# A new step order, a split load of q and a last product in two column halves, in an attention and token-mixing kernel on one core

## The chip, the cores and the metric

The kernel runs on one core of a Trainium2 chip. The metric is the device time of one execution in microseconds (us), lower is better. Times of a kernel are given as the median over several runs, and a separate profiled execution has its own time and a span, which is the part of it that the trace covers. Five engines work in parallel, each through its own queue in program order: PE (TensorE, matrix products, results in PSUM), DVE (VectorE), ACT (ScalarE), POOL (GpSimd) and SP (SyncE, here only for issuing DMAs).

## The reference

Eight batches, eight heads, 576 tokens, head size 64, 32 packing queries. Two attentions one after the other, then a token-mixing layer on the heads laid side by side (x is 576 x 512 in each batch):

```python
p_packed = sm_attn(p, k, v)                # softmax(p k^T / 8) v : 32 x 64 per head
out = sm_attn(q, p_packed, p_packed)       # softmax(q p_packed^T / 8) p_packed
x = out.transpose(0, 2, 1, 3).reshape(B, S, H * D)
W_tok = scale * np.einsum('bsd,btd->bst', x @ w_q, x @ w_k)
mixed = np.einsum('bst,btd->bsd', W_tok, x)
return np.maximum(mixed, 0.0) @ w_out      # 8 x 576 x 512, float32
```

## The kernel before

Inputs are float32 in device memory; POOL's DMAs convert them to bf16 while loading. There is no scheduler: a string named ORDER (line 12) lists all steps, and the program issues them in that order, so each engine's queue is the list cut down to that engine's steps. A step is written as NAME.batch.part@engine=PSUM banks, where V is DVE, A is ACT, P is POOL, S is SP. Semaphores for the data follow from what is read and written; an engine whose next step isn't ready stands still, whatever comes after.

The steps of one batch, in order of data, with the lines of their code:

- LD (157 to 184): LD.k, LD.v (two DMAs), LD.q are the batch's loads; LD.g and LD.h are the two halves of k of batch 0; LD.O is w_out, LD.W the two small weights, LD.P p. All but some of P and W go through POOL's queue. Four buffers each for k, q and v (NL).
- KT (256, DVE): k transposed in 32x32 blocks. S1 (264, PE): p k^T. X1 (288, ACT): exp. TE (296, DVE): transposes that exp, from batch 3 on. PV (301, PE): times v, with a column of ones for the sums. RC, PP (313, 317, DVE): reciprocal, scaling, block mask. PT (322, DVE): transposes the result.
- QK, QKE, QD (327 to 341): p_packed times [w_k, w_q] on PE, its eviction, a copy on POOL.
- QV (347, DVE, three parts): q transposed; parts 0 and 1 each read one half of the q tile, part 2 both. S2 (360, PE): scores of q. X2 (373, ACT): exp. RS, RR (388, 394, DVE), AM (399, DVE or POOL): row sums, reciprocals, product. A number behind the batch picks token tiles (TCH): 3 is the first four tiles of 128, 2 the fifth, 4 all, 0 and 1 two each.
- AT (407, PE) and AE (414): the softmax weights transposed. WKQ (426, PE), WE (449): x w_k and x w_q in one go. GM, GE, Y, YE (454 to 479): a 512-row mixing matrix, reduced to 64 x 128 pieces through p_packed. MX and MR (481, 487, PE): mixed, four token tiles and the remainder. RL, RLF, RLR (508 to 515): relu to SBUF.
- OT (520, PE): relu times w_out, four 128x512 products for each of the token tiles 0 to 3; OT.b.4, for odd b, is the remainder of two batches. OE (538) evicts two tiles at once, OEF (541) one. ST (547) stores two tiles in 512 KB or a remainder in 256 KB; STF (565) one tile in 256 KB.
- HOLD (559): a 128-byte DMA on SP that reads a loaded tile. SP can issue nothing behind it until that load has landed; all stores stand behind it in SP's queue. WARM (588): products on a constant, which keep PE busy while it has no data; 74 of them.

PSUM has eight banks of 512 float32 columns; a step that writes a bank waits until the last reader of it is done.

The loads stand in POOL's queue as g h q0 v0 k1 v1 q1 k2 v2 q2 k3 O v3 q3 k4 q4 v4 k5 q5 v5 k6 v6 q6 k7 q7 v7, with POOL's other steps between. Stores go through SP's queue in the order of the list, but for two STF of the last batch on ACT's queue. PE's list from S1.3 to S1.4, and its end:

```
S1.3 MX.1.0 MR.1 MX.1.1 OT.0.0 OT.1.4 OT.0.1 PV.3 AT.2.3 OT.0.2 AT.2.2 OT.0.3 WKQ.2 S2.3 GM.2 OT.1.2 S1.4
...
MX.7.1 MR.7 MX.7.0 OT.6.3 OT.7.4 OT.7.1 OT.7.3 OT.7.0 OT.7.2
```

Of the kernel before, what the change touches and what calls it, by code (L numbers as in the profile page):

```python
# [7 lines left out]
NL, NB, NO, NE = 4, 3, 6, 2  # L8
# [16 lines left out]
PT.2@V RLR.0@V QV.2.1@V RL.0.1@A WARM.2=1 WKQ.1.0=4,5 WKQ.1.2 WKQ.1.1 S2.2.2=2,3 S2.2.3=6,7 WE.1.2@A
GM.1=4 QK.2=5 KT.3.2@V GE.1@V X2.2.3@A X2.2.2@A Y.1=4 QKE.2@V YE.1@A RS.2.4@V S1.3=6,7,0,1 X1.3.0@A
MX.1.0=4,5 MR.1=2,3 RLR.1@A X1.3.1@A TE.3.0@V RR.2.4@V LD.q4 QD.2@P LD.v4 AM.2.2@P LD.k5 LD.q5
MX.1.1=6,7 OT.0.0=2,3 OT.1.4=0 OT.0.1 RL.1.0@A OE.0.0@A TE.3.1@V AM.2.3@V PV.3.0=4,5 PV.3.1 RL.1.1@V
AT.2.3=1 AE.2.3@A OT.0.2=2,3 AT.2.2=6 AE.2.2@A OEF.1.4@V RC.3.1@V RC.3.0@V OT.0.3 OE.0.1@A PP.3.0@V
QV.3.2@V PP.3.1@V QV.3.1@V PT.3@V QV.3.0@V WKQ.2.0=4,5 KT.4.2@V WKQ.2.2 WKQ.2.1 WE.2.2@A S2.3.3=0,1  # L30
S2.3.2=2,3 X2.3.3@A X2.3.2@A GM.2=6 OT.1.2=4,5 S1.4=0,1,2,3 RS.3.4@V GE.2@A Y.2=6 OT.1.3 X1.4.0@A
X1.4.1@A YE.2@A RR.3.4@V QV.4.0@V TE.4.0@V AM.3.2@P QV.4.2@V TE.4.1@V OT.1.0=0,1 MX.2.1=2,3 QK.3=6
QKE.3@V QV.4.1@V OE.1.1@A MR.2=4,5 RLR.2@A RL.2.1@A OT.1.1 PV.4.0=4,5 PV.4.1 AT.3.2=2 MX.2.0=6,7
OE.1.0@A LD.v5 AM.3.3@P LD.k6 QD.3@P LD.v6 RC.4.0@V RC.4.1@V AT.3.3=3 PP.4.0@V PP.4.1@V PT.4@V
AE.3.3@V AE.3.2@A S2.4.2=4,5 RL.2.0@A X2.4.2@A S2.4.3=0,1 QK.4=6 X2.4.3@A KT.5.2@V QKE.4@A RS.4.4@V
RR.4.4@V WKQ.3.0=4,5 WKQ.3.1 WKQ.3.2 OT.2.0=2,3 S1.5=0,1,6,7 WE.3.2@A X1.5.1@A X1.5.0@A OT.2.2=4,5
OT.2.3 GM.3=0 OT.2.1 LD.q6 AM.4.3@P LD.k7 QD.4@P LD.q7 AT.4.3=1 QV.5.1@V TE.5.0@V TE.5.1@V OE.2.1@A
AM.4.2@V GE.3@V AT.4.2=4 OE.2.0@A Y.3=0 YE.3@A AE.4.2@A QV.5.0@V AE.4.3@V QV.5.2@V PV.5.0=6,7 PV.5.1
MR.3=0,1 MX.3.0=4,5 RLR.3@A RC.5.0@V RC.5.1@V PP.5.1@V PP.5.0@V RL.3.0@A PT.5@V MX.3.1=2,3
WKQ.4.0=0,1 RL.3.1@V WKQ.4.2 WKQ.4.1 S2.5.3=6,7 QK.5=4 S2.5.2=2,3 WE.4.2@A GM.4=5 OT.3.2=0,1  # L40
KT.6.2@V X2.5.3@A X2.5.2@A GE.4@A QKE.5@A RS.5.4@V S1.6=2,3,6,7 Y.4=5 X1.6.1@A OT.3.4=4 OT.3.3
X1.6.0@A YE.4@A OEF.3.4@A TE.6.1@V OE.3.1@A TE.6.0@V RR.5.4@V AM.5.2@V MX.4.0=2,3 MX.4.1=4,5
PV.6.0=6,7 PV.6.1 OT.3.0=0,1 OT.3.1 RL.4.0@A RL.4.1@A LD.v7 QD.5@P AM.5.3@P RC.6.0@V RC.6.1@V
QV.6.1@V PP.6.1@V QV.6.2@V PP.6.0@V QV.6.0@V AT.5.2=2 PT.6@V OE.3.0@A AT.5.3=3 MR.4=4,5 S2.6.3=6,7
S2.6.2=0,1 RLR.4@A X2.6.3@A X2.6.2@A AE.5.2@V AE.5.3@V KT.7.2@V RS.6.4@V WKQ.5.0=2,3 WKQ.5.2 WKQ.5.1
OT.4.0=4,5 WE.5.2@A S1.7=0,1,6,7 OT.4.1 X1.7.0@A OT.4.2=0,1 GM.5=3 RR.6.4@V AM.6.2@P AT.6.2=2 OT.4.3
X1.7.1@A OE.4.0@A AE.6.2@A GE.5@A QK.6=3 Y.5=6 TE.7.0@V QV.7.0@V TE.7.1@V YE.5@V QV.7.1@V QV.7.2@V
PV.7.0=4,5 PV.7.1 RC.7.1@V RC.7.0@V PP.7.0@V PP.7.1@V PT.7@V OE.4.1@A QKE.6@A AM.6.3@P QD.6@P
# [14 lines left out]
def kernel(  # L63
# [11 lines left out]
    nc = tc.nc  # L75
    fp32 = mybir.dt.float32
# [14 lines left out]
    P = 128  # L91
# [529 lines left out]
```

## Time and profile before

| What | us |
|---|---|
| median of 3 runs | 108.7 (108.44 to 111.67) |
| the profiled execution's own time | 109.28 |
| its span | 107.5 |
| PE busy | 94.7 |
| DVE busy | 81.1 |
| ACT busy | 69.1 |
| POOL busy | 41.5 |
| first product with w_out (L533) starts | 40.27 |
| last product ends | 102.34 |

The span lies inside the execution's time; the rest is start and end that the trace does not cover. Page part 2 cuts the span into 40 slices of 2.69 us. A window line names the stretch, its length, then the busy time of the engines asked for with their instruction counts, the TensorE clock granted (1.00 is full), the DMA engines' share and the GB/s moved. In a line of waits the waiting instruction stands left of the arrow, what it waited for stands right, then the us in total, the number of times and the longest. In a timeline line the start and the duration come first, then engine, line, operation, tiles and form. The trace also records when each DMA's sixteen parts have landed; "landed" in this document means the last of them.

### The profile page before, as it was taken

The numbers are of one execution on the slowest core, as the hardware profiler recorded it, in microseconds if no ns is written. First come the engines' busy times: TensorE is split into PE (matmuls) and PEld (weight loads), VectorE is DVE, ScalarE is ACT, GpSimd is POOL, SyncE is SP. The second block draws the span as 40 slices with busy tenths as digits, with TensorE's granted clock in tenths as the row PEclk, the third lists the DMA queues.
The fourth block names the chain that finished last, engine by engine and source line by source line (L and its number), as shares of the span: only waits on it lengthen the run. The fifth ranks groups of instructions, "written<-read, shape, count | busy, mean of one in ns | idle before, by whom it ended". The sixth has DMA issues, their size and how long they took to land.

```text
span 107.5 us, 3573 instructions
## 1 busy us (share of the span) xinstructions
PE 94.7 (88%) x1522; PEld 53.9 (50%) x1542; DVE 81.1 (75%) x161; ACT 69.1 (64%) x105; POOL 41.5 (39%) x65
## 2 busy tenths in 40 slices
PE   2998698998998989979989999999999999999900
PEld 1343545754665644654457566455656565644400
DVE  5135274599798899997989899979997898938500
ACT  4260210542787996878899689899888785658220
POOL 5996138249028046100697492124036040000000
PEclk9999999999999999999999999999999999999996
DMA  2999999999999999999999999999799999955691
GB/s 98 188 154 179 203 212 205 213 212 210 206 211 210 208 206 212 214 208 208 215 210 206 215 204 214 213 213 206 143 369 405 404 396 401 409 213 229 264 380 42
DMA packets 13216, 25.01 MB, mean 233 GB/s; under 512 B 1040, under 2 KB 6160, under 8 KB 13200
## 3 DMA queue, kind: packets, MB, share of 16 engines
q0 software_dynamic: 9344, 14.81, 77.2%
q1 hardware_dynamic: 3520, 9.31, 22.4%
q10 hardware_dynamic: 336, 0.66, 1.7%
q8 instruction: 12, 0.20, 0.7%
q14 instruction: 4, 0.03, 0.1%
HBM read 30.15 MB, written 9.44 MB: 368 GB/s over the span
## 4 chain that ended last, share of the span: by engine, by line
PE 37%; DMA 28%; DVE 19%; issue 5%; POOL 4%; ACT 2%; ACTq 0%; DVEq 0%; POOLq 0%
DMA k_sb<-in_k_dram 28%; PE ps L533 20%; DVE qT L236 4%; PE ps L371 3%; DVE pp L319 3%; PE ps L485 2%; DVE relu L498 2%; DVE e L236 2%; PE ps L439 2%; PE ps L310 2%; PE ps L283 2%; PE ps L460 2%; DVE rec L315 2%; DVE a L403 1%; DVE rs L392 1%
## 5 line engine op out<-in xcount | busy, mean ns | idle before, releaser
L533 PE MATMUL ps<-wout,relu 128*128 128x512 bf16 x115 | 30.0, 380 | 0.8 <-issue 0.2
L403 POOL TENSOR_TENSOR a<-e,rr 128x256 bf16<-128x256 f32 (+2 forms) x10 | 12.9, 1290 | 25.7 <-DVE rr L397 14.7
L588 PE MATMUL ps<-o 128*128 128x512 bf16 x68 | 18.4, 419 | 2.7 <-DVE o L137 2.0
L130 ACT ACTIVATE o<-ps 128x1024 f32<-128x1024 f32 (+1 forms) x15 | 14.5, 969 | 6.6 <-PE ps L533 6.4
L533 PEld LDWEIGHTS <-relu 128*128 128x128 bf16 x128 | 11.2, 98 | 11.9 <-issue 1.4
L376 ACT ACTIVATE e<-ps 128x256 f32<-128x256 f32 (+2 forms) x17 | 10.8, 674 | 8.1 <-PE ps L371 7.7
L496 ACT ACTIVATE relu<-ps 128x1024 bf16<-128x1024 f32 (+1 forms) x12 | 14.5, 1233 | 1.1 <-PE ps L485 1.1
L236 DVE STREAM_TRANSPOSE qT<-q_sb 128x512 uint32<-128x512 uint32 (+1 forms) x24 | 13.0, 552 | 2.2 <-DMA q_sb<-in_q_dram 2.1
L236 DVE STREAM_TRANSPOSE kT<-k_sb 128x1152 uint32<-128x1152 uint32 (+1 forms) x9 | 11.2, 1246 | 3.6 <-DMA k_sb<-in_k_dram 3.4
L392 DVE TENSOR_REDUCE rs<-e 128x40 f32<-128x1280 f32 (+2 forms) x10 | 12.0, 1210 | 1.8 <-ACT e L376 1.6
L588 PEld LDWEIGHTS <-o 128*128 128x128 bf16 x74 | 7.1, 105 | 11.0 <-issue 3.2
L178 POOL DMA_DIRECT2D v_sb<-in_v_dram x16 | 10.0, 636 | 4.5 <-DVE v_sb L208 4.0
L371 PE MATMUL ps<-ppT,qT 64*128 64x64 bf16 x320 | 7.0, 190 | 1.4 <-DVE qT L236 0.5
L310 PE MATMUL ps<-v_sb,e 64*64 64x192 bf16 x288 | 7.9, 245 | 0.2
L130 ACT ACTIVATE aT<-ps 128x128 bf16<-128x128 bf16 (+2 forms) x10 | 5.1, 536 | 4.5 <-PE ps L412 4.5
L371 PEld LDWEIGHTS <-qT 64*128 64x128 bf16 x320 | 6.1, 94 | 3.8 <-DVE pp L319 1.3
L132 POOL COPY pqk<-pqk 128x128 bf16<-128x128 bf16 x8 | 2.4, 294 | 14.0 <-ACT pqk L130 6.2
L236 DVE STREAM_TRANSPOSE e<-e1T 128x576 bf16<-128x576 bf16 x10 | 7.3, 744 | 0.4 <-ACT e1T L294 0.3
L130 ACT ACTIVATE wkq<-ps 128x896 bf16<-128x896 f32 (+1 forms) x8 | 7.0, 873 | 0.8 <-PE ps L439 0.8
L310 PEld LDWEIGHTS <-e 64*64 64x64 bf16 x288 | 6.0, 106 | 2.6 <-issue 1.1
L294 ACT ACTIVATE e1T<-ps 128x576 bf16<-128x576 f32 x10 | 6.1, 649 | 1.8 <-PE ps L283 1.7
L498 DVE TENSOR_SCALAR relu<-ps 128x1024 bf16<-128x1024 f32 (+1 forms) x6 | 6.5, 1108 | 0.6 <-ACT e L376 0.3
(68 smaller groups left out, 143.1 us busy)
## 6 DMA issues: line engine op xcount, KB each, us to landing
out_dram<-o SPq DMA_DIRECT2D x14, 512.0 KB, 5.6
q_sb<-in_q_dram POOLq DMA_DIRECT2D x8, 576.0 KB, 14.1
v_sb<-in_v_dram POOLq DMA_DIRECT2D x16, 288.0 KB, 13.0
k_sb<-in_k_dram POOLq DMA_DIRECT2D x7, 576.0 KB, 14.1
out_dram<-orem SPq DMA_DIRECT2D x4, 256.0 KB, 3.9
k_sb<-in_k_dram POOLq DMA_DIRECT2D x2, 288.0 KB, 6.8
wout<-in_moe_w_out_dram POOLq DMA_DIRECT2D x1, 512.0 KB, 14.9
out_dram<-o ACTq DMA_DIRECT2D x2, 256.0 KB, 3.6
```

The source lines that it names most:

```text
L130: nc.scalar.activation(o, i, COPY)
L178: nc.gpsimd.dma_start(v_bufs[b % NL][halves(i), 1:5], src)
L236: nc.vector.transpose(o, i)
L310: nc.tensor.matmul(T["pv", b][halves(cc), i, cc * Dh:(cc + 3) * Dh], lhsT, rhs, start=n == 0, stop=n == R - 1, skip_group_check=True)
L371: nc.tensor.matmul(ps[:, y, t - t0, i], lhsT, rhs, start=e == 0, stop=e == 1)
L376: nc.scalar.activation(e2[:, t0:t1].rearrange("a t (i y n) -> a y (t i) n", i=2, y=2), T["s2", b, c].rearrange("a y t i n -> a y (t i) n") ...
L392: nc.vector.tensor_reduce(rs[:, t0 * H:t1 * H], src, axis=AX, op=ADD)
L403: e.tensor_tensor(a2[:, t0:t1].rearrange("a t i (u l) -> a (t i u) l", l=L), e2v(b, c), T["rr", b][:, t0 * H:t1 * H].to_broadcast((P, (t1 ...
L496: nc.scalar.activation(o, i, RELU)
L498: nc.vector.tensor_scalar(o, i, 0.0, None, op0=MAX)
L533: nc.tensor.matmul(ps, lhsT, wout[:, j, :], start=j == 0, stop=j == NJ - 1)
L588: nc.tensor.matmul(ps, warm[:, 0:P], warm, start=True, stop=True)
```

## The change

Five things change at once.

1. q of batch 7 is loaded by two DMAs: LD.q7 its second half, LD.r7 its first; they now come last, behind v7.
2. HOLD waits for v7 instead of q7.
3. All stores are issued by SP; the two STF on ACT's queue are gone.
4. Token tile 3 of batch 7 is computed by OH in two halves of 256 columns, evicted by OEH and stored by STH in 128 KB each; the second half is PE's last step.
5. ORDER is written anew: steps stand in another order on every engine, and some are given to another engine.

The loads' order in POOL's queue is now h g v0 q0 k1 v1 q1 k2 v2 q2 k3 O k4 v3 q3 v4 q4 k5 q5 v5 k6 q6 v6 k7 v7 q7 r7. Steps that change engine are, off DVE: QKE.1, QKE.3, GE.0, RL.1.1, OEF.1.4, AE.3.3, AE.5.2, YE.5, YE.6, GE.6 and OE.5.0 to ACT, AM.0.3, AM.4.2, AM.5.2, AM.7.1 and AM.7.2 to POOL; onto DVE: PC, PB.1.0, WE.0.2, WE.6.2, RLR.1 to RLR.4, AE.2.3, AE.7.1, GE.2, GE.5, GE.7, YE.3, YE.4 and OEF.5.4 from ACT, AM.0.2, AM.1.2, AM.2.2, AM.7.0 and PB.0.0 from POOL; and the two copies WC from ACT to POOL. RL.5.0 and RL.5.1 swap engines, as do the four RLF, and OEF.7.0, 7.2 and 7.4. The third load on SP, P1, came on ACT's queue before. The warm-up products are again 74, spread otherwise.

```diff
--- before
+++ after
@@ ORDER, the stretch around the first products with w_out, and the end
...
+GM.1=6 GE.1@V WARM.1=3 S1.3=6,7,4,5 Y.1=0
+QKE.2@V X1.3.1@A YE.1@A X1.3.0@A RS.2.4@V OT.0.0=2,3 MX.1.1=4,5 MX.1.0=6,7 OT.0.1 OT.0.2=0,1
...
+KT.4.2@V WE.2.2@A RLR.1@V PV.3.1 GM.2=5 S1.4=2,3,0,1 RC.3.1@V RC.3.0@V OT.1.4=4 PP.3.1@V
+GE.2@V PP.3.0@V PT.3@V X1.4.1@A X1.4.0@A Y.2=1 QK.3=7 OT.1.2=2,3 YE.2@A QKE.3@A OEF.1.4@A QV.3.1@V
+QV.3.0@V QV.3.2@V S2.3.2=6,7 S2.3.3=0,1 MX.2.1=4,5 X2.3.2@A X2.3.3@A TE.4.1@V TE.4.0@V MR.2=6,7
...
+HOLD.v7 ST.1.4 ST.3.4 ST.0.1 ST.4.1 ST.1.1 ST.0.0 ST.2.0 ST.3.0 ST.3.1 ST.4.0 OEF.5.4@V GE.7@V
+ST.1.0 ST.2.1 ST.5.0 ST.5.4 ST.5.1 OE.6.0@A ST.6.0 Y.7=1 YE.7@V OT.6.2=2,3 MX.7.1=0,1 MR.7=6,7
+RLF.7.1.1@A MX.7.0=4,5 RLR.7@V OT.6.3 OT.7.4=6 RLF.7.0.1@A RLF.7.1.0@V RLF.7.0.0@V OH.7.0=4 OT.7.2=5
+OT.7.1=0 OT.7.0=1 OH.7.1 OE.6.1@A OEF.7.2@V OEH.7.0@A OEF.7.4@A OEF.7.1@A OEF.7.0@A OEH.7.1@A ST.6.1
+STH.7.0 ST.7.4 STF.7.2 STF.7.1 STF.7.0 STH.7.1
...
@@ load
+        elif x == "r7":
+            nc.gpsimd.dma_start(q_in[7 % NL][:, 0], pairs(q, 7)[:, 0])
+        elif x == "q7":
+            nc.gpsimd.dma_start(q_in[7 % NL][:, 1], pairs(q, 7)[:, 1])
...
+    def OH(b, h, eng, bk=None):
+        if bk is not None:
+            T["otf", b, 3] = bank(bk, [D])
+        ps = T["otf", b, 3][:, h * 256:(h + 1) * 256]
+        for j in range(NJ):
+            nc.tensor.matmul(ps, T["relu", b][:, j // 2, j % 2, 3 * P:4 * P], wout[:, j, h * 256:(h + 1) * 256],
+                             start=j == 0, stop=j == NJ - 1, skip_group_check=True)
+
+    def OEH(b, h, eng, bk):
+        cs = slice(h * 256, (h + 1) * 256)
+        copy(eng, new("o", b, [P, 4, D], fp32, bufs=NO)[:, 3, cs], T["otf", b, 3][:, cs])
+
+    def STH(b, h, eng, bk):
+        q = nc.scalar if eng == "A" else nc.sync
+        c0 = 3 * D + h * 256
+        q.dma_start(orows(b)[:, :, c0:c0 + 256], T["o", b][:, 3, h * 256:(h + 1) * 256])
```

## The prediction

> **What bounds the kernel now.** I read the slices first, then busy time in 5 us windows, then what TensorE (PE) waits for, then the timeline of the end.
>
> ```profile
> span 107.5 us, 3573 instructions
> PE 94.7 (88%) x1522; PEld 53.9 (50%) x1542; DVE 81.1 (75%) x161; ACT 69.1 (64%) x105; POOL 41.5 (39%) x65
> GB/s 98 188 154 179 203 212 205 213 212 210 206 211 210 208 206 212 214 208 208 215 210 206 215 204 214 213 213 206 143 369 405 404 396 401 409 213 229 264 380 42
> ```
>
> The GB/s row has two floors: about 210 (loads, counted as bf16 written) from slice 4 to slice 27, then about 400 (stores). Loading saturates the queues until about 77 us. The landing records give k3 at 36.8 us, wout at 39.9, q3 at 44.9, k7 at 73.0, q7 at 76.0 and v7 at 78.8: 2.85 us for each tensor of a batch.
>
> ```profile
> 36.00:41.00 5.00, 4.38 (x116) 1.00 1.20 210
> 41.00:46.00 5.00, 4.95 (x63) 1.00 1.10 209
> 46.00:51.00 5.00, 4.40 (x110) 1.00 1.16 209
> 51.00:56.00 5.00, 4.61 (x69) 1.00 1.12 212
> ...
> 91.00:96.00 5.00, 4.95 (x52) 1.00 0.77 303
> 96.00:101.00 5.00, 4.95 (x29) 1.00 0.61 244
> sum 65.00, PE 62.13; mean PE 4.78
> ```
>
> These windows show PE alone (window, length, busy time, granted clock 1.00). From 36 to 101 us it is idle for only 65.00 - 62.13 = 2.87 us, and the warm-up products (L588) all lie before. So PE bounds everything after wout lands; before that, the loads set when it gets real work. A new order can win at most those 2.87 us there.
>
> ```profile
> PE ps L371 <- DVE qT L236: 0.5, 1, 0.5
> PE ps L371 <- DVE ppT L236: 0.4, 2, 0.3
> PE ps L485 <- ACT e1T L294: 0.3, 1, 0.3
> ```
>
> The named waits are few: S2.3 at 47.1 us waits for the transposes of q3, MX.1.1 at 39.7 for ACT. The rest are gaps under 0.2 us.
>
> ```profile
> 101.42 1.35 SPq L567 DMA_DIRECT2D out_dram<-o  x2
> 102.37 0.60 ACT L130 ACTIVATE o<-ps 128x512 f32<-128x512 f32 x1 [1.99 <-PE ps L533]
> 103.00 0.55 ACTq L567 DMA_DIRECT2D out_dram<-o  x1
> ```
>
> The end is a chain: the last product ends at 102.34, its eviction takes 0.60, the last store is issued at 103.00, lands 3.27 us later (landing record 106.27), and the span closes 1.2 us after that.
>
> **The change part by part.** This profiled execution took 109.28 us with a span of 107.48, 0.58 above the median of 108.7. I sum changes against the span and apply the result to the median.
>
> *Start, until k3.* The same tensors are loaded before k3, and the number of warm-up products is 74 in both. v0 now goes ahead of q0, so PV.0 moves from 16.3 to about 14 us. That buys nothing: S1.1 waits for k1, which lands at 19.2 in both. POOL's new work (WC, a 128x1024 AM.0.3 at 1.96 us instead of 0.61) stands ahead of LD.O (issued at 24.99 before, about 24.8 now), behind four tensors not yet landed, 11 us of backlog. The new conversion on DVE (PC, 1.06 us on ACT before; 0.5 to 1.1 bounds it) and P1 as third on SP put PX at about 6.6 to 7.6 instead of 5.94; S1.0 waits for k0 at 10.3 anyway. POOL's wait there (PB.0.2) has LD.v1 behind it, but four tensors are in flight. Bounds -0.3 to +0.4, taken 0. If the backlog were gone, each us here would come through whole.
>
> *wout's landing.* Before, PE did MX.1.0, MR.1 and MX.1.1 (0.75 us) between S1.3 and OT.0.0, which starts at 40.27. Now OT.0.0 stands right behind S1.3 and Y.1, ready at about 39.1, and wout lands at 39.9: PE idles 0.8 us, less the old 0.28, less 0.3 since OT.0.0 starts earlier: +0.45 behind, having skipped 0.75 of work.
>
> *The middle, 40 to 77.* I walked the new list by hand: PE's groups at their durations (one OT 0.87, PV 0.87, S2 0.78, WKQ 0.8 to 0.9, GM 0.35, one MX 0.3), each held by its producer's in-order queue (DVE: KT 1.3, RS 1.45, two TE 1.4, the three QV 1.55, RL 1.28; ACT: RL 1.3, OE 1.0, WE 0.9, X2 1.3), and compared work done at equal times.
> - End of S2.3 (50.8 us): +0.2. The 0.55 us hole before S2.3 goes. K4 now goes ahead of v3 and q3, so v3 lands at 39.9 + 2 x 2.85 = 45.6 (PV.3 fits at 45.6) and q3 at 48.45; DVE reaches QV.3 at 48.3 to 48.5. GM.2 waits 0.15 for WE.2, behind OE.0.1 on ACT.
> - End of S2.4 (57.4): -0.25. The gaps of 51 to 56 (0.39) mostly go.
> - End of WKQ.4 (66.0): +0.15; WKQ.3 waits 0.3 for AE.3, which moved to ACT behind X2.4.3.
> - End of WKQ.5 (76.9): 0. S2.6.2 waits for RL.4.0 on ACT, OT.3.1 follows it closely.
>
> Work moved between DVE and ACT here cancels: off DVE QKE.3 0.41, RL.1.1 1.30, OEF.1.4 0.67, AE.3.3 0.65, AE.5.2 0.2 and two AM 0.88 (4.1 us); onto it four RLR 1.6, AE.2.3 0.65, GE.2 and GE.5 0.57, two YE 0.85, AM.2.2 0.44 (4.1 us). POOL takes the AM; its loads q6 to k7, issued by about 58 us, have 8 us of backlog ahead.
>
> *q7 in two transfers, v7 ahead.* One more POOL issue (0.58, as the half k loads of L161), on a queue that waits for QD.5 behind it with nothing due. v7 lands at about 75.9 instead of 78.8, r7 at about 78.8. PV.7 in the new list stands behind OT.4.1, at 81 us, and QV.7 behind TE.7, at 80: neither uses its early data. Taken 0; if stores delay r7, the cover is 2 us (QV.7.2 at about 80.9).
>
> *HOLD by v7.* SP's 23 stores queue behind it; they start at about 75.9 instead of 76.02. Stores are not the limit: GB/s falls to 213 in slice 35, when they wait for evictions. 0.
>
> *Tail to OT.6.3.* From WKQ.5 on, before took 76.94 to 97.86: 20.92 us, some 0.6 idle. The same groups remain. New waits: GM.6 behind WE.6.2, which moved to DVE behind RL.5.0 (1.3 + 1.1 us from PT.7 at 84.0: ready at 86.45, PE there at 86.2): 0.3. Others that I find have slack (MR.7 waits for OE.6.0: 0.3 slack; AT.7: 1 us). Between -0.4 (no gap) and +0.5, taken +0.1.
>
> *Last products.* OT.7.3 becomes two groups of four 256-column products. L439 (256 columns) has spacing of about 0.11 beside 0.22 for 512, so PE time is equal to within 0.1. The last eviction shrinks from 0.60 to 0.38 (the 128x256 row), but ACT must first end OEF.7.0, 0.1 to 0.2 late, and SP needs 0.55 for each issue: STF.7.0 at MR.7's end + 5.8, STH.7.1 at + 6.35. Before, the last issue stood at 103.00, with MR.7 ending at about 96.65: also + 6.35. What remains is the landing: 512 KB stores on an idle queue landed in 2.98 to 3.17 us, 256 KB in 3.19, so size alone shows no gain; but the last one landed in 3.27 behind its forerunner, and half of it queues half as long. Between 0 and -0.4, taken -0.2.
>
> The Trainium skill's page "DMA: Bandwidth & Descriptors", section "Anatomy of one DMA", fits about 2.0 us fixed plus bytes at 436 GB/s; 131,072 bytes less would be worth 0.3 us by it, and the sum 0.1 lower. The trace's fixed part agrees in kind (about 3 us at two sizes); it shows no size term.
>
> Sum: 0 + 0 (middle, lag at 76.9) + 0.1 - 0.2 = -0.1 us: 108.7 - 0.1 = **108.6 us**. Steps' bounds give 107.4 (all gaps down to a third: -1.1, tail -0.2) to 109.7 (the wout hole 0.45, start 0.4 and the waits found 0.15 all kept).
>
> **Rivals.**
> 1. *Slower: q3 comes late.* Its landing (48.45) and its use (48.3 to 48.5) meet without slack, where before it had landed 0.7 us ahead of its first transpose (45.6). QV.3 stands at the head of DVE's in-order queue, before TE.4, RS.3 and RC.4, and PE's S2.3 right after; so each us of delay is a us at the end. For: the landings' parts spread by 2.9 us over the 16 queues from k3 on, and q2 to k3 took 3.93 us instead of 2.85. Against: the rate is even after. At one spread late, +2.5: 111.2 us. It decides beyond 2% from q3 landing later than 50.7.
> 2. *Faster: the new order closes nearly all gaps.* Of the 2.87 us, about 0.8 remain, since 75 to 101 us had that with no named wait: -2.1, tail -0.2: 106.4 us. Against: the waits that I found above.
> 3. *POOL and DVE block each other.* The 128x256 product on POOL took 1.58 us beside DVE's 128x1024 one, and 0.61 alone; it ended 0.48 after DVE did. AM.0.2/AM.0.3 and AM.7.0/AM.7.1 now run as such pairs: 0.75 in the last softmax, partly uncovered, and 0.6 earlier: 109.3 us. Against: AT.7 has 1 us of slack. The Trainium skill's page "SBUF — State Buffer", section "SBUF: two separate sides", calls this an exclusive lock in which the loser blocks for the whole instruction; by that rule these pairs run one after the other, and the 1.58 agrees.
> 4. *The change does not do what it says: the stores let go by v7 take bandwidth from r7.* 2.2 us of loads remain at 76.6; at half rate they end at 81.0, 0.1 after use. 108.8 us; beyond 2% only if r7 lands after 83.
>
> **How the numbers follow.** Forecast 0.62; rival 1 0.17, rival 2 0.10, rival 3 0.07, rival 4 0.04. The likeliest's own range is 107.4 to 109.7; to leave out no more than 2 in 10, the range takes in half of rivals 1 and 2: 106.9 to 110.9. 2%, about what a measurement of this kernel can tell from no change, is 2.2 us: faster (under 106.5) is the better part of rival 2, 0.08; slower (over 110.9) most of rival 1 and a little besides, 0.16; within 2% 0.76.
>
> **What would show it.** PE idle right before the first L533 of the new profile (0.8 us) shows the wout step; DVE idle by q_sb near 48 us, with S2.3 after it, shows rival 1; PE idle from 36 to 101 us between 2 and 3.3 us shows the balance; v7's landing 2.9 us ahead of the last q7 part, with no DVE idle near 81, shows that part to be free; the last issue 6.3 us after MR.7 shows the tail. The forecast is wrong if the idle sum there leaves 1 to 4.5 us, or if k3 or wout land over 1 us off.

## The result, and the profile after

| What | before | after |
|---|---|---|
| median, us | 108.57 (4 runs) | 113.07 (112.56 to 113.30, 4 runs) |
| profiled execution, its span, us | 109.28, 107.5 | 113.3, 111.5 |
| S1.0, the first useful products, starts | 11.55 | 12.20 |
| first product with w_out starts | 40.27 | 42.40 |
| last product ends | 102.34 | 104.50 |
| last product's end to the span's end | 5.14 | 7.0 |

The changed kernel is slower: 1.0415 times the time before, 95% interval 1.0366 to 1.0463. Of the 4.0 us of span, 2.16 are there when PE ends and 1.86 come behind it. Of 28 executions of the kernel before that ran beside e9 to e12, six took 111.0 to 111.6 us at a mean granted clock of 0.975 to 0.977, the others had 0.986 to 1.00; ratios leave these out, as any execution over 1.5% above the fastest of its kernel.

The page of the changed kernel: span, busy times, PE's busy tenths and clock by slices of 2.79 us, GB/s.

```profile
span 111.5 us, 3603 instructions
PE 97.7 (88%) x1546; PEld 55.6 (50%) x1546; DVE 80.6 (72%) x165; ACT 68.1 (61%) x102; POOL 43.1 (39%) x66
PE   5994699968989899999999899999999999999400
PEclk9999769999999999999999999999999999999985
GB/s 48 164 159 202 213 211 205 211 212 208 214 212 209 207 209 213 205 212 212 211 213 207 209 210 209 208 209 159 285 106 331 401 397 406 376 345 215 84 318 152
```

PE's row has a 4 in the fourth slice and the clock's row a 7 and a 6 in the two slices after it: an idle stretch, then a slow PE. At the other end PE is done two and a half slices before the span ends, and GB/s falls to 84 there before the stores' last burst.

The sum of PE's windows of the changed kernel from 36 to 101 us, as shown of before:

```profile
sum 65.00, PE 63.62; mean PE 4.89
```

From 36 to 101 us PE now idles 1.38 us instead of 2.87. So the new order does what an order can do there; the loss lies at the two ends. The start, first the changed kernel, then the kernel before (PE's timeline: start, duration, line, products, idle ahead of it and its releaser; L611 and L588 are the warm-up products):

```profile
1.19 8.32 PE L611 MATMUL ps<-o 128*128 128x512 bf16 x28 [1.19 <-DVE o L138]
12.20 2.08 PE L278 MATMUL ps<-pblk,kT 128*64 128x128 bf16 x36 [2.69 <-DVE kT L241]
14.21 1.98 PE L611 MATMUL ps<-o 128*128 128x512 bf16 x5
16.12 0.94 PE L315 MATMUL ps<-v_sb,e 64*64 64x192 bf16 x36
16.98 3.19 PE L611 MATMUL ps<-o 128*128 128x512 bf16 x14
20.11 0.78 PE L376 MATMUL ps<-ppT,qT 64*128 64x64 bf16 x40
20.82 1.90 PE L611 MATMUL ps<-o 128*128 128x512 bf16 x8
```

```profile
2.03 8.44 PE L588 MATMUL ps<-o 128*128 128x512 bf16 x28 [2.03 <-DVE o L137]
11.55 1.25 PE L273 MATMUL ps<-pblk,kT 128*64 128x128 bf16 x36 [1.09 <-DVE pblk L134]
12.96 3.40 PE L588 MATMUL ps<-o 128*128 128x512 bf16 x15 [0.16 <-issue]
16.30 0.94 PE L310 MATMUL ps<-v_sb,e 64*64 64x192 bf16 x36
```

PE idles 2.69 us ahead of S1.0 instead of 1.09, for two reasons. The 28 warm-up products begin 0.84 us earlier, since DVE now fills their constant (SET.warm) as its first step, and end at 9.51 instead of 10.47. And S1.0 starts 0.65 us later; in this trace the half of k0 that it needs lands at 11.34 instead of 10.29. Then the same 36 products take 2.08 instead of 1.25 us, and five warm-up products 1.98. The windows of PE at that place, after and before, say why:

```profile
10.00:12.00 2.00, 0.00 (x0) 1.00 1.20 204
12.00:14.00 2.00, 1.80 (x36) 0.58 1.15 213
14.00:16.00 2.00, 2.00 (x11) 0.57 1.11 212
16.00:18.00 2.00, 2.00 (x42) 1.00 1.11 209
```

```profile
10.00:12.00 2.00, 0.91 (x19) 1.00 1.09 199
12.00:14.00 2.00, 1.84 (x33) 1.00 1.19 203
```

The granted clock falls to one half for 3.41 us from 12.3 on. And nothing behind it absorbs the delay: the 22 warm-up products between PV.0 and QK.0 (3.19 + 1.90 us) stand in PE's queue, whatever is late. By S1.1 PE is 2.3 us behind (23.00 against 20.70). The chain of work of the changed kernel (page part 4, by engine):

```profile
PE 67%; DVE 10%; DMA 7%; ACT 7%; issue 2%; POOL 2%; ACTq 0%; POOLq 0%; DVEq 0%
```

against that line for the kernel before:

```profile
PE 37%; DMA 28%; DVE 19%; issue 5%; POOL 4%; ACT 2%; ACTq 0%; DVEq 0%; POOLq 0%
```

The chain now runs through PE almost from the start, 9% of the span through warm-up products alone; the wait for loads that the prediction leant on is down from 28% to 7%.

The end, ACT's and then SP's timeline of the changed kernel:

```profile
104.54 0.39 ACT L131 ACTIVATE o<-ps 128x256 f32<-128x256 f32 x1 [3.30 <-PE ps L575]
104.82 0.59 ACT L131 ACTIVATE orem<-ps 128x512 f32<-128x512 f32 x1
105.30 1.37 ACT L131 ACTIVATE o<-ps 128x512 f32<-128x512 f32 x3
```

```profile
104.95 0.54 SPq L585 DMA_DIRECT2D out_dram<-o  x1
105.58 0.54 SPq L556 DMA_DIRECT2D out_dram<-orem  x1
106.22 1.85 SPq L589 DMA_DIRECT2D out_dram<-o  x3
108.16 0.56 SPq L585 DMA_DIRECT2D out_dram<-o  x1
```

The first line is OEH.7.0, the eviction of the first column half. Its products ended at about 101.5, but ACT idles 3.30 us ahead of it, until the second half (L575 again) is done at 104.5: both halves lie in bank 4, and OH.7.1 stands ahead of OEH.7.0 in the list, so the eviction is ordered behind the second half's write. The evictions of the remainder, of two whole tiles and of the second half stand behind it in ACT's queue, and behind the first half's store come five more, which SP hands over 0.64 us apart. The Trainium skill's page "PSUM — Partial Sum Buffer", section "PSUM bank collisions raise a hardware error", tells the programmer to guard PSUM by bank and quadrant, not by address; the 3.30 us agree with such a guard when the list has the halves in this order. Whether the program guards the bank or the tile that both halves belong to, no run here shows.

### The profile page after: what moved, and what is told of

The parts are those of the page before. It is cut to its first block, busy times and chain, and to the rows that moved or that the text cites. A ratio compares the mean times of both kernels' runs of the same rounds, so it can differ in the third digit from the quotient of the medians.

```text
span 111.5 us, 3603 instructions
## 1 busy us (share of the span) xinstructions
PE 97.7 (88%) x1546; PEld 55.6 (50%) x1546; DVE 80.6 (72%) x165; ACT 68.1 (61%) x102; POOL 43.1 (39%) x66
## 4 chain that ended last, share of the span: by engine, by line
PE 67%; DVE 10%; DMA 7%; ACT 7%; issue 2%; POOL 2%; ACTq 0%; POOLq 0%; DVEq 0%
PE ps L538 23%; PE ps L611 9%; DMA k_sb<-in_k_dram 7%; PE ps L315 6%; PE ps L376 4%; PE ps L278 4%; PE ps L417 4%; PE ps L490 3%; PE ps L444 3%; PE ps L439 3%; DVE qT L241 3%; PE ps L465 2%; ACT e L381 2%; DVE kT L241 2%; PE ps L337 2%
## 5 line engine op out<-in xcount | busy, mean ns | idle before, releaser
L538 PE MATMUL ps<-wout,relu 128*128 128x512 bf16 x124 | 30.3, 380 | 0.0
L408 POOL TENSOR_TENSOR a<-e,rr 128x1024 bf16<-128x1024 f32 (+2 forms) x11 | 13.8, 1258 | 25.6 <-DVE rr L402 17.0
L611 PE MATMUL ps<-o 128*128 128x512 bf16 x74 | 20.7, 426 | 2.4 <-ACT e L296 1.2
L131 ACT ACTIVATE o<-ps 128x1024 f32<-128x1024 f32 (+2 forms) x18 | 16.0, 911 | 5.8 <-PE ps L575 3.3
L501 ACT ACTIVATE relu<-ps 128x1024 bf16<-128x1024 f32 (+1 forms) x13 | 15.7, 1232 | 1.2 <-PE ps L496 0.6
L538 PEld LDWEIGHTS <-relu 128*128 128x128 bf16 x124 | 10.9, 98 | 11.0 <-issue 0.5
L611 PEld LDWEIGHTS <-o 128*128 128x128 bf16 x74 | 7.4, 107 | 11.9 <-issue 5.4
L241 DVE STREAM_TRANSPOSE qT<-q_sb 128x512 uint32<-128x512 uint32 (+1 forms) x24 | 12.3, 547 | 0.0
L320 DVE RECIPROCAL rec<-ps 64x2 f32<-64x2 f32 x16 | 2.7, 167 | 8.2 <-PE ps L315 8.0
L296 ACT ACTIVATE e<-ps 128x1152 bf16<-128x1152 f32 x3 | 3.4, 1132 | 6.7 <-PE ps L278 6.7
L131 ACT ACTIVATE aT<-ps 128x128 bf16<-128x128 bf16 (+1 forms) x10 | 4.8, 506 | 4.0 <-PE ps L417 3.9
L278 PE MATMUL ps<-pblk,kT 128*64 128x128 bf16 x108 | 4.6, 249 | 2.7 <-DVE kT L241 2.7
```

The lines of the kernel that those rows point to most:

```text
L131: nc.scalar.activation(o, i, COPY)
L241: nc.vector.transpose(o, i)
L278: nc.tensor.matmul(ps_all[halves(i), bk[r // 3], r % 3 * P:(r % 3 + 1) * P], kT[:, i, r, :, e], pblk[:, 2 * b + i, :, :, e].rearrange("a c ...
L408: e.tensor_tensor(a2[:, t0:t1].rearrange("a t i (u l) -> a (t i u) l", l=L), e2v(b, c), T["rr", b][:, t0 * H:t1 * H].to_broadcast((P, (t1 ...
L501: nc.scalar.activation(o, i, RELU)
L538: nc.tensor.matmul(ps, lhsT, wout[:, j, :], start=j == 0, stop=j == NJ - 1)
```

## The experiments

**The two ends, first four runs.** Theory: 1.86 us from the blocked eviction, 2.16 from a start in which PE, not the loads, decides. Rivals: SP's many issues; the halves as such; late loads.

e1, the first half's eviction ahead of the second half's products:

```diff
-OT.7.1=0 OT.7.0=1 OH.7.1 OE.6.1@A OEF.7.2@V OEH.7.0@A OEF.7.4@A
+OT.7.1=0 OT.7.0=1 OE.6.1@A OEH.7.0@A OH.7.1 OEF.7.2@V OEF.7.4@A
```

> The changed kernel with one move in ORDER: OE.6.1 and OEH.7.0 stand ahead of OH.7.1 in the list, so that the first half's eviction is not made to wait for the second half in the same PSUM bank. Theory bank: in the changed kernel ACT stood 3.30 us before OEH.7.0 (start 104.54, the end of OH.7.1), and three more evictions and six store issues were queued behind it. Freed, OEH.7.0 starts at about 101.5, OEH.7.1 ends at about 105.1 and the last issue stands at about 105.4 instead of 108.16: the span falls by 2.5 to 2.8 us, the time from 113.1 to about 110.4. Rival SP: the six last stores, 0.64 us apart on one queue, set the end whatever the evictions do: less than 0.6 us.

Measured: 110.57 us, ratio 1.0150 (1.0049 to 1.0252). ACT's timeline:

```profile
102.24 0.38 ACT L131 ACTIVATE o<-ps 128x256 f32<-128x256 f32 x1 [0.28 <-PE ps L575]
102.52 0.59 ACT L131 ACTIVATE orem<-ps 128x512 f32<-128x512 f32 x1
103.97 0.60 ACT L131 ACTIVATE o<-ps 128x512 f32<-128x512 f32 x1 [0.85 <-PE ps L538]
104.83 0.87 ACT L131 ACTIVATE o<-ps 128x512 f32<-128x512 f32 x2 [0.27 <-PE ps L538]
```

ACT now idles 0.28 instead of 3.30 us ahead of this eviction, and PE's end to the span's end is 4.4 instead of 7.0 us: 2.6 us, with all stores still on SP. The rival, that the number of SP's issues made the tail long, falls with it.

e2, tile 3 whole again (OT.7.3, OEF.7.3, STF.7.3 for the halves), the rest of the tail as in the changed kernel:

```diff
-OH.7.0=4 OT.7.2=5
-OT.7.1=0 OT.7.0=1 OH.7.1 OE.6.1@A OEF.7.2@V OEH.7.0@A OEF.7.4@A OEF.7.1@A OEF.7.0@A OEH.7.1@A ST.6.1
-STH.7.0 ST.7.4 STF.7.2 STF.7.1 STF.7.0 STH.7.1
+OT.7.3=4 OT.7.2=5
+OT.7.1=0 OT.7.0=1 OE.6.1@A OEF.7.2@V OEF.7.3@A OEF.7.4@A OEF.7.1@A OEF.7.0@A ST.6.1
+STF.7.3 ST.7.4 STF.7.2 STF.7.1 STF.7.0
```

> The changed kernel with token tile 3 of the last batch as one product group of 512 columns, one eviction on ACT and one store on SP, in the place of the first half; all else of the change kept. Theory bank: no wait of 3.3 us, last product, then 0.60 us eviction, then one issue: the span falls by 2.2 to 2.6 us, 0.2 less than with halves whose eviction is freed. Rival SP: with five instead of six stores at the end it falls by 0.6 us.

Measured: 110.73 us, 1.0119 (0.9994 to 1.0245), tail 4.45 us beside 4.42 in e1. Halves with a free eviction and a whole tile cannot be told apart.

e2's start is the changed kernel's, step by step, and its trace shows that start at the full clock:

```profile
1.19 9.11 PE L611 MATMUL ps<-o 128*128 128x512 bf16 x28 [1.19 <-DVE o L138]
12.01 1.24 PE L278 MATMUL ps<-pblk,kT 128*64 128x128 bf16 x36 [1.71 <-DVE kT L241]
```

Its first product with w_out starts at 40.73 instead of 42.40; 0.19 of that is S1.0's start, so the halving alone is worth about 1.5 us. It is usual with this start, but not certain: of the 12 executions of the changed kernel, e1 and e2, this one has a mean clock of 0.993, the others 0.966 to 0.984. Nor is k0 the only thing that holds S1.0: here its half landed at 10.28, as early as before, but DVE came to transpose it only at 11.20, after its work on p, whose third load on SP landed at 6.57.

e3, more warm-up ahead of S1.0:

```diff
-WARM.28=0 S1.0=1,2,3
+WARM.40=0 S1.0=1,2,3
```

> The changed kernel with 40 instead of 28 warm-up products at the start, which fill the 2.69 us in which PE stood still before S1.0 (9.51 to 12.20) and after which the granted clock was 0.5 for 3.4 us. Theory clock: S1.0 takes 1.25 instead of 2.08 us and WARM.5 1.1 instead of 1.98, PV.0 starts at about 14.6 instead of 16.12, S2.0 at about 18.4 instead of 20.11, and as the chain up to the first product with w_out is of PE work and its followers, all behind comes 1.3 to 1.8 us earlier: about 111.5 us. Rival loads: the chain is held by k0, v1 and k2 as they land, so that the gain is gone by S1.1: 0 to 0.4 us.

Measured: 112.15 us, 1.0301 (1.0200 to 1.0402). In the profile the clock stays full, S1.0 starts at 12.00 and takes 1.25 us, the first product with w_out starts at 40.76 instead of 42.40, PE ends at 102.9 instead of 104.5: 1.6 us come through to the end. The medians differ by 0.9 us. So 12 products more give the start that e2's trace had at the full clock.

e4, the small loads at the start as before (P1 on ACT's queue, then W0, P0, W1 on SP):

```diff
-LD.P0@S LD.W0@S LD.P1@S LD.P2 LD.P3
+LD.P1@A LD.W0@S LD.P0@S LD.W1@S LD.P2 LD.P3
...
-LD.k1 LD.W1@S
+LD.k1
```

> The changed kernel with the small loads as before: P1 on ACT's queue, W0, P0, W1 on SP at the start. Theory loads: the second half of k0 lands at 10.3 instead of 11.34, S1.0 starts 1 us earlier, PE's idle time before it falls from 2.69 to 1.7 us, and the half clock may not come: 1.0 to 2.5 us off the span. Theory clock alone: the halving came after 2.8 us of idle, so it goes with it or stays; if it stays, PV.0 is only 1 us earlier and the end by 0.5 to 1 us.

Measured: 111.28 us, 1.0156 (1.0021 to 1.0291). S1.0 starts at 11.01, with 1.28 us of idle time ahead of it and the full clock; S1.1 then waits 0.87 us for k1's transposes, and the first product with w_out starts at 40.69, within 0.1 us of e3. So of S1.0's earlier start only the clock is worth something.

**What remains of the start.** e5 is e3 with the five warm-up products ahead of PV.1 in another bank: bank 3 lies between banks 1 and 7 that X1.1 reads with one strided instruction, and PE waited 1.22 us there for ACT's exp.

```diff
-X1.1.0@A WARM.5=3 PV.1.0=6,7
+X1.1.0@A WARM.5=0 PV.1.0=6,7
```

> The changed kernel with 40 warm-up products at the start, and with the five ahead of PV.1 in PSUM bank 0 instead of 3. Theory wait of the padding: with bank 3 these five waited for X1.1 to end (1.22 us idle, then 1.17 us of products) and stood between X1.1 and PV.1; in bank 0 they run beside X1.1, PV.1 starts at about 23.8 instead of 25.00, the first product with w_out at about 39.6 instead of 40.76 us, and the time is 0.8 to 1.2 us under that of the kernel with 40 warm-up products alone (112.15). Rival loads: v1 and k2 set PV.1 and S1.2, so the first product with w_out starts within 0.3 us of 40.76.

Measured: 111.76 us, 1.0233 (1.0153 to 1.0314). PV.1 starts at 24.10 instead of 25.00, the first product with w_out at 39.90 instead of 40.76, but PE ends only 0.2 us earlier than in e3: between 56 and 61 us PE is busy 4.01 instead of 4.50 us, with 0.88 us ahead of AT.4 that no wait in the profile explains.

e6 is e3 without any of the warm-up products behind S1.0 (three of the places are shown):

```diff
-X1.0.0@A WARM.5=0 PV.0.0=2,3
+X1.0.0@A PV.0.0=2,3
...
-KT.1.2@V WARM.14=1 S2.0.3=2,3
+KT.1.2@V S2.0.3=2,3
...
-RS.0.4@V WARM.8=1 QK.0=3
+RS.0.4@V QK.0=3
...
```

> The changed kernel with 40 warm-up products at the start and none of the other 46. Theory padding on the path: WARM.14 and WARM.8 stand between PV.0 and S1.1 (5 us of products), the fives ahead of PV.1 and WKQ.0, the four ahead of PV.2; without them S2.0 starts at about 17.5 to 18, S1.1 at 20.7 to 21.0, PV.1 at 23.5, and the first product with w_out 1.2 to 2 us earlier than with them, at 39 to 39.6 us: 110.5 us. Theory clock: in the holes PE is idle for most of some microseconds at a time, the granted clock falls to 0.5 again (it did after 2.7 us of idle time in the changed kernel), for 3.4 us or more each time, and the first product with w_out comes no earlier or later than 40.76 us.

Measured: 114.73 us (112.81 to 117.61), mean clock 0.875 to 0.921. PE's windows:

```profile
15.00:20.00 5.00, 1.31 (x68) 0.93 1.15 208
20.00:25.00 5.00, 3.34 (x61) 0.50 1.13 212
25.00:30.00 5.00, 3.88 (x58) 0.50 1.18 210
30.00:35.00 5.00, 4.72 (x98) 0.50 1.11 210
35.00:40.00 5.00, 4.21 (x56) 0.52 1.17 209
```

The clock is halved for 20.5 us, though PE is 67 to 94% busy in the windows from 20 us on. The warm-up products are thus a price that is paid on PE's path to keep the clock; without them the first product with w_out comes at 44.13.

e7 is e5 with the first eviction of WKQ on ACT as before:

```diff
-WE.0.2@V
+WE.0.2@A
```

> As the kernel with 40 warm-up products and the five in bank 0, with WE.0.2 on ACT again, as before the change. Theory DVE queue: WE.0.2 (1.09 us) stood in DVE's queue ahead of KT.2, on which S1.2 waits, while k2 had landed at 28.1; without it S1.2 starts about 1 us earlier, and the first product with w_out 0.5 to 1 us earlier than with WE.0.2 on DVE. Rival: by S1.3, 9 us later, k3's landing at 36.5 and the chain behind S2.1 have taken it up: within 0.2 us.

Measured: 110.88 us, 1.0154 (1.0079 to 1.0229); first product with w_out at 39.96, as in e5. The rival in its expectation was right for the start. Between 56 and 61 us PE is busy 4.50 us again, and it ends 0.2 us earlier.

e8 is the kernel before with the new loads of batch 7: q7 in two transfers, v7 ahead of them, HOLD by v7.

```diff
-LD.q7 AT.4.3=1
+AT.4.3=1
...
-LD.v7 QD.5@P
+LD.v7 LD.q7 LD.r7 QD.5@P
...
-HOLD.q7
+HOLD.v7
```

> The kernel before with two of the five parts alone: q of the last batch in two transfers, last in the queue behind v7, and HOLD by v7; the list is otherwise that of before. Forecast of the document: no change, within 0.3 us, since PV.7 and QV.7 stand behind other work. Rival stores: stores let go 2.9 us ahead of the last load slow r7; QV.7, S2.7 and the end come later by the delay beyond 79.5 us, up to 2 us.

Measured: 109.57 us, 1.0038 (0.9993 to 1.0084). These parts of the change cost nothing that the runs can see.

**Do the parts add up?** e9 is e1 and e3 together. e10 has all repairs: e1, e4's loads, e5's bank, e7's engine, and 34 warm-up products ahead of S1.0:

```diff
-WARM.28=0 S1.0=1,2,3
+WARM.34=0 S1.0=1,2,3
```

> The changed kernel with both repairs at once: the first half's eviction stands ahead of the second half's products, and 40 instead of 28 warm-up products stand ahead of S1.0. Theory (the change's +4.02 us of span is a tail of +1.86 from the blocked eviction and a start that the halved clock and the padding made late): the two repairs add up. The eviction repair alone took the ratio to the kernel before from 1.0415 to 1.015, the warm-up repair alone to 1.030, so together 1.0035; range 0.997 to 1.010, PE end near 103.0, PE end to span end near 4.5 us. Rival A (they overlap: one hides the other, since the last stores or loads set the end): not under 1.012. Rival B (something else in the new order costs more than 1 us besides): over 1.010 although clock and tail are repaired.

> All that the runs showed to cost, taken out of the changed kernel: eviction of the first half ahead of the second half's products, old order of the small loads with 34 warm-up products ahead of S1.0, the five warm-up products ahead of PV.1 in bank 0 instead of 3, WE.0.2 on ACT. Theory (the rest of the new order is worth about 0.7 us between the first products with w_out and OT.6.3, and nothing else is wrong with it): first L538 near 39.9 to 40.2 although 0.75 us of MX.1 now stands behind it, PE end 102.2 to 102.6, tail 4.5; ratio 0.985 to 1.003. Rival (the loads pace the middle, so that an earlier start is given back at the waits for k and v): same start, PE end not before 102.8, ratio over 1.003.

Measured: e9 109.79 us, 1.0029 (0.9984 to 1.0075): start and tail account for the loss, and their repairs add up (1.0035 expected); in e9's trace PE still ends 1.28 us later than before, 0.72 of it by S1.0's start, and the tail is 0.8 us shorter. e10 **107.68 us, 0.9897 (0.9861 to 0.9933)**: with its ends mended the changed kernel is the faster one. Its first product with w_out starts at 39.76, PE ends at 102.2, 0.1 us earlier than before, and the tail is 4.1 us: of the 1.1 us of span that it gains, 1.0 lie behind PE's end. This split is that of one pair of traces: e15 and e18 below, whose lists are e10's but for the last store or the last tile, end PE at 101.18 and 101.63, and e8, e12 to e14 and e16, variants of the kernel before, at 101.67 to 103.69. In its 11 timed executions the mean clock is 0.993 to 1.00, in the four of the changed kernel 0.966 to 0.969.

e11 goes the other way: the kernel before with 16 instead of 28 warm-up products ahead of S1.0.

```diff
-WARM.28=3 S1.0=0,1,2
+WARM.16=3 S1.0=0,1,2
```

> The kernel before with 16 instead of 28 warm-up products ahead of S1.0, nothing else; PE then idles some 3.5 us ahead of S1.0 instead of 1.1. Clock theory: the granted clock falls to about 0.5 for 3.4 us or a multiple of it from about S1.0 on, S1.0 takes 2.0 to 2.1 us instead of 1.25, the warm-up products behind it take twice as long, first L533 at 41.3 to 42.0 instead of 40.27, PE end and time +1.0 to +1.7 us (ratio 1.009 to 1.016). Rival (as the prediction had it, the loads set the early steps, and what PE does ahead of wout's landing is covered): S1.1 still starts within 0.3 us of 20.7, first L533 within 0.4 of 40.27, ratio under 1.004.

Measured: 110.59 us, 1.0147 (1.0081 to 1.0214). PE's windows:

```profile
10.00:12.00 2.00, 0.13 (x4) 1.00 1.11 205
12.00:14.00 2.00, 1.68 (x36) 0.57 1.19 205
14.00:16.00 2.00, 1.99 (x6) 0.57 1.16 214
```

It has the changed kernel's halved clock at the same place, a mean clock of 0.977 to 0.986 in all six timed executions, and PE ends 1.9 us later, 0.3 of it by S1.0's own start (11.87). S1.1 starts at 22.58 instead of 20.70. That the loads cover PE's early work is refuted in the kernel before itself.

**What are the halves worth, and why is the mended tail shorter than the old one?** With the eviction free, PE's end to the span's end is 4.1 to 4.45 us against 5.14 before, with halves and without. e12 puts only the halves into the kernel before, first eviction free; e13 only has its two STF issued by SP; e14 does both; e15 gives the last store of e10 to ACT.

```diff
@@ e12, the kernel before
-OT.7.3=2 OT.7.0=3 OT.7.2=5 ST.4.1 ST.5.1 ST.5.0 OEF.7.4@V ST.6.0
-OEF.7.3@V OEF.7.0@V OEF.7.1@A ST.6.1 ST.7.4 STF.7.1@A STF.7.3 OEF.7.2@A STF.7.0 STF.7.2@A
+OH.7.0=2 OT.7.0=3 OT.7.2=5 OEF.7.4@V OEH.7.0@V OEF.7.0@V OH.7.1 ST.4.1 ST.5.1 ST.5.0 ST.6.0
+OEF.7.1@A ST.6.1 ST.7.4 STF.7.1@A STH.7.0 OEF.7.2@A STF.7.0 OEH.7.1@V STF.7.2@A STH.7.1
@@ e13, the kernel before
-STF.7.1@A STF.7.3 OEF.7.2@A STF.7.0 STF.7.2@A
+STF.7.1 STF.7.3 OEF.7.2@A STF.7.0 STF.7.2
@@ e15, e10
-STF.7.0 STH.7.1
+STF.7.0 STH.7.1@A
```

> The kernel before with only the column halves: tile 3 of batch 7 as two halves, the first in the place of OT.7.3 and evicted by DVE ahead of the second half's products, the second as PE's last step, stored in 128 KB; the other evictions and stores keep their engines but for DVE evicting the second half. Theory (the halves are sound once the eviction is free): PE end unchanged at 102.3, the last eviction 0.38 instead of 0.60, the last issue 0.2 us earlier, the last landing 0.2 to 0.6 us earlier since 128 KB landed 0.1 to 0.4 us faster than 256 KB in the runs; ratio 0.994 to 0.999. Rival (an own price of the halves: two more groups, evictions and stores, or the store ahead of the last one lands last): ratio 1.000 to 1.006.

> The kernel before with its two STF on ACT's queue issued by SP instead, nothing else. Queue theory (stores that alternate between two queues land later: 3.27 to 4.0 us after issue with the sixteen parts spread over 0.9 to 1.1 us in the kernel before and in its version with halves, against 2.4 to 2.6 us and a spread of 0.2 in the changed kernel's versions, at the same 3.9 us from the first to the last issue): last issue as before about 0.65 us after PE's end, landing 2.4 to 2.6 us behind it, PE end to span end 4.3 to 4.5 instead of 5.14; ratio 0.990 to 0.996. Rival (the landing is set by the bytes that queue up, not by the queue): landing 3.2 to 3.4, ratio 0.998 to 1.004.

> The same with the column halves besides, the first half's eviction free. If the halves are worth the shorter last eviction (0.42 instead of 0.60) and the smaller last store (128 KB landed 2.1 to 2.2 us after issue, 256 KB 2.4 to 2.6), PE end to span end is 3.9 to 4.2 and the ratio 0.003 to 0.005 under that of the kernel with one queue alone. If SP's spacing of 0.64 us for each issue or the eviction queue eats it, the two agree within 0.002.

> The changed kernel with all repairs, but its last store (128 KB) issued by ACT right behind its eviction. It is then issued 0.3 to 0.4 us earlier, since SP's spacing of 0.64 us no longer stands ahead of it. Queue theory: it lands 2.9 us or more after its issue instead of 2.13, so PE end to span end grows from 4.2 to 4.5 or more and the ratio to before from 0.990 to 0.993 or more. Rival (the queue does not matter): landing 2.1 to 2.2, PE end to span end 3.8 to 3.9, ratio 0.986 to 0.988.

Measured: e12 1.0026 (0.9987 to 1.0064), e13 0.9983 (0.9936 to 1.0031), e14 0.9980 (0.9924 to 1.0035), e15 107.64 us, 0.9836 (0.9782 to 0.9891). Stores of the last tiles (page part 6: count, KB each, median us from issue to landing), in the kernel before, e13 and e10:

```profile
out_dram<-o SPq DMA_DIRECT2D x2, 256.0 KB, 3.5
```

```profile
out_dram<-o SPq DMA_DIRECT2D x4, 256.0 KB, 3.5
```

```profile
out_dram<-o SPq DMA_DIRECT2D x3, 256.0 KB, 2.5
```

One queue leaves the 3.5 us as they are, so the queue theory falls; e15's last store landed 2.47 us after its issue on ACT's queue, neither 2.9 nor 2.1; issued 0.35 us earlier, it left the tail at 4.2 us. Counted from PE's end, the last landing comes 3.94 us later in the kernel before, 3.91, 3.92 and 3.90 in e12, e13 and e14, and 3.26, 2.98 and 2.98 in e1, e10 and e15. The times show no gain of the halves in either family.

e16 and e17 sought the difference in the tail's order, e18 is e10 with a whole tile 3.

```diff
@@ e16, the kernel before, all stores on SP
-ST.6.1 ST.7.4 STF.7.1@A STF.7.3 OEF.7.2@A STF.7.0 STF.7.2@A
+ST.6.1 STF.7.1 STF.7.3 ST.7.4 OEF.7.2@A STF.7.0 STF.7.2
@@ e17, the kernel before
-OT.7.4=4 OT.7.1=0 OE.6.1@A OT.7.3=2 OT.7.0=3 OT.7.2=5
+OT.7.4=4 OT.7.3=0 OT.7.2=2 OT.7.1=3 OT.7.0=5 OE.6.1@A OEF.7.2@V OEF.7.3@A OEF.7.4@A OEF.7.1@A OEF.7.0@A
...
```

> The kernel before with all stores on SP and the remainder's store (ST.7.4, 256 KB) behind the stores of tiles 1 and 3 instead of right behind ST.6.1 (512 KB). Burst theory (1 MB handed over within 1.3 us builds up about 1 us of writes that the later stores, 0.65 to 0.8 us apart at 400 GB/s, never let drain): ST.6.1 is then followed by a gap of 1.2 us as in the changed kernel, the last store lands 2.4 to 2.7 us after its issue instead of 3.26, PE end to span end 4.4 to 4.6; ratio 0.991 to 0.997. Rival (it is which tiles are written last, 0 and 2, or something before the tail): landing 3.2 to 3.3, ratio 0.997 to 1.002.

> The kernel before with the changed kernel's tail: tiles 3, 2, 1, 0 of batch 7 whole and in that order, their evictions on the engines and in the order of the changed kernel, all stores by SP. Theory (the order of tail's products, evictions and stores is what shortens it): PE end as before near 102.3, PE end to span end 4.3 to 4.5 instead of 5.1; ratio 0.990 to 0.996. Rival (something earlier in the changed order, such as when the stores begin, sets the landing): PE end to span end 5.0 to 5.2, ratio 0.998 to 1.003.

> The changed kernel with all repairs, and tile 3 whole instead of in halves. If the halves are worth nothing, as the pair e1 and e2 left it within the noise: PE end to span end 4.2 to 4.4, ratio within 0.003 of the mended kernel with halves (0.984 to 0.990). If they are worth the smaller last store: 0.2 to 0.4 us longer, ratio 0.989 to 0.993.

Measured: e16 0.9993 (0.9950 to 1.0036), last landing 3.92 us after PE's end: the burst theory falls too. e17 111.73 us, 1.0230 (1.0173 to 1.0286), tells nothing: in its list OE.6.1 stands behind products that write the same banks 2 and 3, so it waits for them and evicts their values for two tiles of batch 6. e18 107.93 us, 0.9892 (0.9838 to 0.9946), as e10: in time the whole tile does as well as the halves. Its tail is 4.40 us, e10's 4.14.

## Why the prediction was wrong, by its steps

The forecast was 108.6, range 106.9 to 110.9. Two of its terms failed, both at the ends; the middle, on which nearly all its care was spent, was about right.

1. **Start, until k3: taken 0, bounds -0.3 to +0.4. Measured +2.9.** (The first product with w_out is 2.13 us late, and 0.75 us of MX.1 that stood ahead of it is still to do.) The step said that what PE does early "buys nothing" or costs nothing, since loads set the pace ("S1.1 waits for k1"), and "each us here would come through whole" only if the backlog were gone. The tensors did land as said or sooner: k3 at 36.47, wout at 38.99, 0.3 and 0.9 us earlier than before. But they were not what PE waited for. PE's queue was full of warm-up products that nothing shortens, and ahead of them the earlier end of the first 28 and the later S1.0 let PE idle long enough to halve its clock. The kernel before is paced by PE there too: in its trace and those of e8, e12 to e14, e16 and e17, which share its start, S1.0 starts at 10.89 to 12.11 us and S1.1 always 9.11 to 9.15 us later, though k1 lands anywhere from 1.47 to 1.96 us ahead of S1.1. By experiments: 1.64 us are the idle time and the halved clock (e3, and e2's trace; e11 shows the same from the other side, with no part of the change in it), about 0.86 the bank of five warm-up products (e5), though little of that came through to PE's end. Where the remaining 0.4 us lie is not shown: e4 and e7, beside e3 and e5, moved the first product with w_out by less than 0.1 us, and S1.0's start differs by 1.2 us among those seven traces of one start. e10 is 0.24 us behind by the same count. The prediction counted 74 warm-up products in both kernels and stopped there; it should have asked when those ahead of S1.0 begin and how far the last of them ends from k0's transposes. PX, put at 6.6 to 7.6, started at 7.30, but at 8.63 in e2 and e3, where it was DVE and not k0 that held S1.0.
2. **wout's landing: PE idles 0.8 us. Not seen**, no idle time stands ahead of the first L538, since PE came 3.4 us after wout. The mended kernels, whose PE is on time, do not show it either: in e10, e15 and e18 wout lands 0.69 to 0.86 us ahead of the first product with it (38.90 and 39.76 in e10). The step took wout's landing, 39.9, from one trace; in e8, e13, e14 and e16 it lands at 38.34 to 38.62, in e12 at 40.41. Its own terms, 0.8 less 0.28 less 0.3, also give 0.2 and not 0.45.
3. **The middle and the tail to OT.6.3: -0.35 us between wout and OT.6.3 (0.45 to 0.1). Measured -0.7** in the changed kernel (2.9 us behind at the first product with w_out, 2.16 at the last) and -0.37 in e10, which is on time (-0.19 and -0.38 in e15 and e18). The sum of the hand-made walk through the queues held; as it started from the 0.45 of step 2, which had not come, some of that is luck. Of the waits that it found, WKQ.3's for AE.3 on ACT came, at 62.44 us, 0.40 for the 0.3 that it took; those of GM.2 and GM.6 do not show.
4. **q7 in two transfers, HOLD by v7: 0. Right**, by e8: 1.0038, interval across 1. v7 landed 2.76 us ahead of the last part of q7, as said (2.9).
5. **Last products: -0.2. Measured +1.86.** The step reckoned that STH.7.1 would be issued 6.35 us after MR.7's end; it was 9.2 (98.99 to 108.16). (Before, it was 6.17 and not 6.35: MR.7 ended at 96.83, not at 96.65.) It took OEH.7.0 for free as soon as its four products ended. The names gave it away: both halves are slices of one bank, and the list has OH.7.1 ahead of OEH.7.0. That costs 2.6 us (e1); against it stand 0.7 to 1.0 us by which the last stores land earlier, which the step did not foresee. The gain of the smaller store, taken at 0.2, shows in no time (e2, e12, e14, e18); in the traces the tail is 0.03 to 0.26 us shorter with halves than without (e1 against e2, e10 against e18). The fit that the prediction cited from the Trainium skill, with 0.3 us for the smaller store, is given there for DMAs that GpSimd issues, and SP issues this one; the landings in the changed kernel agree with it (2.19 us for the last 128 KB, 2.50 for the 256 KB ahead of it), e15's last 128 KB, at 2.47, does not.

The wait of WKQ.3, as it stands among PE's waits in the changed kernel:

```profile
PE ps L439 <- ACT aT L131: 0.4, 1, 0.4
```

None of the rivals came: q3 landed at 47.69 and PE was busy for all of 46 to 51 us (rival 1); the gaps did close by half (rival 2) but outweighed; the last softmax's pairs on POOL and DVE are hidden, with PE busy for all but 0.01 us from 76 to 96 us (rival 3); r7 landed at 79.53 (rival 4). The list lacked the one that mattered, a start decided by PE. The signs to look for were half right: the one at the end (last issue 6.3 us after MR.7) showed the fault at once, the ones for the start (k3 or wout over 1 us off) watched the loads, where little had changed. PE's idle time from 36 to 101 us, 1.38, also missed the 2 to 3.3 that was to show the balance.

What stays open: why the last stores land 3.9 us after PE's end in the kernel before and its variants, and 3.0 to 3.3 in those of the changed kernel whose eviction is free. Queue, halves and the remainder's place are excluded by e12 to e16; the order of the tiles was not tried soundly, since e17's list overwrites values of batch 6.

## What to carry to other kernels

Where products on a constant keep PE busy, they are work on PE's path like any other: look at when the last of them ends and when the first data land, and at the granted clock in that window, before calling an early step covered by loads. When two instructions share a PSUM bank, the list's order between the write of one part and the read of the other decides who waits, so evict the first part ahead of the next write. Closing the gaps in the middle won 0.2 to 0.7 us here; one blocked eviction at the end cost 2.6.

## What the runs showed of the hardware

- The clock is granted in steps: by the trace's clock records, the stretches at one half last 3.41 us (the changed kernel, e11), 6.83 (e1) and 20.48 (e6). The Trainium skill's page "TensorE: Matmul & The Clock Gate", part 1, gives a free-running window of 3413 ns; all these are one, two and six of them. It lets the clock fall after a window without work; here a window with 0.72 us of work (8.89 to 12.30 in the changed kernel) was enough, and in e6 stretches of 5 us of which 67 to 94% were busy did not restore it.
- How much idle time halves the clock? The stretches at full clock are whole multiples of 3.41 us too (6.83, 92.16, 98.99), so a trace can be cut into stretches of 3.41 us at its clock's steps. In the 20 traces each such stretch with 1.33 us of products or less ended with the fall to one half (0.43 us in e11, 0.72 in the changed kernel, 0.78 and 1.33 in e6, 1.25 in e1), and each with 1.65 or more kept the full clock (around S1.0: 1.72 in e12, 1.91 in e2, 2.17 in the kernel before). So the limit lies between 1.33 and 1.65 of 3.41 us here, and one idle time counts by where it falls in these stretches.
- The kernel before is near that limit at S1.0, which may be why six of its 28 executions have the mean clock of e11's trace, 0.975 to 0.977. That these are the same event is read from their mean clock alone; they have no trace.
- The last four stores of the kernel before have the last of their sixteen parts land 0.9 to 1.1 us behind the first, those of e10 0.2 us. In the kernel before, e12 to e14 and e16 this begins about when the trace's DMA records have an 8 KB transfer on a queue of the kind instruction, within 0.6 us of PE's end; in e10 the like comes 3.3 us before it, and in e1 6.3 us. It coincides; that it is the cause was not tried.
